# Linear attention with an MLP: q's features by a transpose of the first product instead of a second product, from unit 8 on

## The chip, the cores and the metric

The kernel runs on one core of a Trainium2 chip. The metric is the device time of one execution in microseconds (us). Before the change it is 369.69 us, the median of three runs (369.42 to 370.6).

## The reference

```
proj = q @ w_phi                      # 8 batches, 8 heads, 576 tokens, 64 -> 128 features; k the same
proj = proj - max |proj|              # a maximum of each token
q_p, k_p = [exp(proj), exp(-proj)]    # 256 features each
kv = k_p^T v;  z = sum of k_p over the tokens
x = (q_p kv) / (q_p z + 1e-6)         # heads side by side: 8 x 576 x 512
xn = (x - mean) / sqrt(var + 1e-6) * g_ln
out = x + relu(xn @ w_ch1) @ w_ch2    # 512 -> 2048 -> 512
```

Inputs and output are float32. The kernel multiplies in bfloat16 and sums in float32.

## The kernel before, in words

**Units and pairs.** The eight batches form four pairs. A pair has eight units, one for two heads of one batch, so there are 32 units, numbered 0 to 31, and units 8 to 31 belong to pairs 1 to 3. The 576 tokens of a head are four tiles of 128 and a tail of 64; the two heads of a unit make eight full tiles and one mixed tile. When the attention of a pair is far enough, its 1152 tokens (nine tiles of 128) go through the layer norm and the MLP in three groups of tiles: (4, 3, 2) in pairs 0 to 2, (3, 3, 3) in pair 3. The first group needs the pair's first four units, the others the second four.

**A unit of attention.** q and k are cast to bfloat16 and transposed, for the first eight units on TensorE and later by a DMA transpose of nine tiles on SP's queue (`a_trans_dma`, L755; its issue is L791, its result `qkT`). Then three kinds of products with `w_phi` follow:

- `main_products` (L880, the products at L885 and L891): tokens on the partitions, features along the row, for k and for q. `maxima` (L948, reduce at L953) takes the maximum of each token on DVE. For k, two exps on ACT (L967) make the features `EB`; for q only the maximum was needed.
- `tail_products` (L896, the products at L900), which the change speaks of as the second product: q again, with features on the partitions and tokens along the row. Two exps on ACT (L1033) make `EA`, the form in which the numerator needs q's features.
- `a_mixed` (L803): the mixed tile, in both forms, with exps of its own (L835, L839).

From unit 4 on (`tiled`) the products of the first two kinds use 64 of TensorE's 128 rows, since a head has 64 dimensions, and are issued in groups by `a_group` (L919) that take both A banks of PSUM at once. Two units share three groups: g1 has k and q of the even unit, g2 the even unit's second product and the odd unit's k, g3 the odd unit's q and its second product. An A bank is 1024 float32 wide. It comes free when its last reader is done: k's after the second exp, q's first product after the maximum, the second product after its second exp.

Then POOL scales v by exps of the maxima (`scale_main`, L974), `a_kv` (L1051, products at L1059 and L1065) sums k's features times v, and `a_num` (L1100, products at L1125, L1133 and L1139) makes numerator and denominator in two parts; part 0 takes an A bank from pair 1 on. DVE scales and adds (L1155, L1161) and inverts (L1167), and POOL writes the quotient into `x` (L1242, L1175; the first units write from DVE). `x` has three buffers, one for each pair in turn.

**The MLP.** `x` is centred (L1330 on DVE, L1335 on ACT, L1340 on POOL) and transposed, in pair 0 on TensorE and from pair 1 on by a DMA transpose on SP's queue (`x_trans_dma`, L1290, issue L1296; its result `xT`). `first` (L1383, products L1389) multiplies by the first matrix, and a ReLU on ACT (L1400) or DVE (L1398) empties the B bank. `second` (L1449, products L1458) multiplies by the second matrix, and ACT (L1471) with POOL (L1477), or DVE alone (L1466), adds `x` and leaves an output tile for SP to store (L1362, L1371). `x` is thus read until a pair's last output tile is made.

**The order of the work.** Each engine, and SP's DMA queue, works through a fixed list in order. `Order.run` (L229) makes these lists when the program is built: every step has a planned duration, what it reads and writes, the PSUM banks that it takes or gives back, and a rank, which is how late it may start, counted back from the MLP's due times, plus an offset from the table `OFF` (L38) by stage and kind of step. Whenever an engine of the plan is free, it takes the ready step with the lowest rank. The first rows of `OFF` are for units 0 to 7 one by one, the others for spans of four units. In the plan a DMA transpose of n tiles holds SP for at least 1.3 us. While the plan has nothing for PE in its first 75 us, it puts in products of zeros (L1665), the filler.

Of the kernel before, what the change touches and what calls it, by code (L numbers as in the profile page):

```python
# [17 lines left out]
def bcast(ap: bass.AP, dim: int, n: int) -> bass.AP:  # L18
# [15 lines left out]
TILED = 4  # L34
FOLD = 4
# [4 lines left out]
        "load": 291.2, "trans": 484.1, "trans.copy": -195.4, "mixed": 341.2, "mixed.max": 116.4,  # L40
        "mixed.exp": 189.4, "mixed.fold": -404.3, "k": -3.8, "k.max": 215.0, "k.em": -118.9,
        "k.exp": 583.1, "en": -216.0, "vv": -100.4, "q": 65.3, "q.max": -159.0, "q.em": 255.7,
        "tails": 174.6, "tails.exp": -410.3, "kv": 6.5, "kv.copy": 79.0, "num0": 131.7,
        "num1": -968.2, "num.dve": -227.8, "g1": 0.0, "g2": 0.0, "g3": 0.0, "put": 717.2,
# [3 lines left out]
        "load": 291.2, "trans": 511.8, "trans.copy": -106.8, "mixed": 340.9,  # L48
        "mixed.max": -109.0, "mixed.exp": 164.3, "mixed.fold": -181.6, "k": -0.3,
        "k.max": -400.0, "k.em": -20.9, "k.exp": 125.3, "en": -151.3, "vv": -156.9, "q": -49.0,  # L50
        "q.max": 314.4, "q.em": 304.2, "tails": 151.0, "tails.exp": -391.2, "kv": 141.9,
        "kv.copy": -46.4, "num0": 0.7, "num1": 201.4, "num.dve": -650.0, "g1": 0.0, "g2": 0.0,
        "g3": 0.0, "put": -13.8, "ln": 223.3, "w1": -144.2, "w2": -136.8, "ln.c": -23.8,
        "ln.t": -23.8,
    },
    {
        "load": 291.2, "trans": 438.4, "trans.copy": 145.2, "mixed": 324.3, "mixed.max": -85.1,
        "mixed.exp": 161.8, "mixed.fold": 14.6, "k": -20.8, "k.max": -401.0, "k.em": 78.2,
        "k.exp": -37.2, "en": -240.5, "vv": -112.4, "q": 149.6, "q.max": -212.7, "q.em": 595.0,
        "tails": -126.8, "tails.exp": -55.8, "kv": -164.2, "kv.copy": -20.3, "num0": -1.2,  # L60
        "num1": 340.4, "num.dve": -181.6, "g1": 0.0, "g2": 0.0, "g3": 0.0, "put": 44.6,
        "ln": -23.8, "w1": -144.2, "w2": 20.3, "ln.c": -23.8, "ln.t": -23.8,
    },
    {
        "load": 291.2, "trans": 101.5, "trans.copy": -4.0, "mixed": 268.3, "mixed.max": -90.8,
        "mixed.exp": 90.4, "mixed.fold": 174.0, "k": 8.8, "k.max": -396.2, "k.em": 243.2,
        "k.exp": -294.7, "en": -302.0, "vv": -102.0, "q": -15.0, "q.max": 52.5, "q.em": 236.8,
        "tails": 368.4, "tails.exp": -384.7, "kv": 383.3, "kv.copy": -55.5, "num0": 431.0,
        "num1": -539.1, "num.dve": -231.8, "g1": 0.0, "g2": 0.0, "g3": 0.0, "put": 225.4,
        "ln": -14.1, "w1": -144.2, "w2": -136.8, "ln.c": 107.3, "ln.t": 102.1,  # L70
    },
    {
        "load": 316.8, "trans": 376.2, "trans.copy": -87.1, "mixed": 51.8, "mixed.max": -100.8,
        "mixed.exp": 164.7, "mixed.fold": -36.7, "k": 556.5, "k.max": 202.3, "k.em": 295.2,
        "k.exp": -167.4, "en": -276.9, "vv": -79.3, "q": 110.5, "q.max": 328.5, "q.em": 303.8,
        "tails": 326.2, "tails.exp": -216.9, "kv": 149.0, "kv.copy": 26.7, "num0": 833.5,
        "num1": -731.1, "num.dve": -351.0, "g1": 137.0, "g2": 17.7, "g3": -5.0, "put": 614.2,
# [3 lines left out]
        "load": 6.3, "trans": -355.5, "trans.copy": -99.1, "mixed": 457.5, "mixed.max": 103.0,  # L81
        "mixed.exp": 265.5, "mixed.fold": 170.2, "k": -2.1, "k.max": -335.5, "k.em": -146.7,
        "k.exp": 597.3, "en": 0.0, "vv": -167.9, "q": 84.5, "q.max": 451.8, "q.em": 568.9,
        "tails": 184.4, "tails.exp": -231.7, "kv": -244.6, "kv.copy": -5.9, "num0": 974.5,
        "num1": -583.9, "num.dve": -219.9, "g1": -233.9, "g2": -41.7, "g3": 81.5, "put": -107.6,
        "ln": 61.6, "w1": -341.2, "w2": -67.5, "ln.c": 107.2, "ln.t": 107.2,
    },
    {
        "load": 544.7, "trans": 446.6, "trans.copy": 285.4, "mixed": 170.0, "mixed.max": -148.7,
        "mixed.exp": 58.0, "mixed.fold": -156.9, "k": -85.8, "k.max": 114.2, "k.em": 74.9,  # L90
        "k.exp": 606.5, "en": -36.5, "vv": -101.1, "q": -87.9, "q.max": 444.8, "q.em": 402.4,
        "tails": 124.7, "tails.exp": -331.1, "kv": 122.4, "kv.copy": 30.0, "num0": 311.2,
        "num1": 336.1, "num.dve": -226.1, "g1": -219.3, "g2": 21.1, "g3": -5.0, "put": 133.8,
# [3 lines left out]
        "load": 6.3, "trans": 477.2, "trans.copy": 113.9, "mixed": 187.6, "mixed.max": 54.3,  # L97
        "mixed.exp": 95.1, "mixed.fold": -78.3, "k": -1.2, "k.max": 94.8, "k.em": 77.7,
        "k.exp": -15.1, "en": -138.5, "vv": -247.2, "q": 144.6, "q.max": 497.6, "q.em": 422.9,
        "tails": 71.6, "tails.exp": -522.1, "kv": 195.5, "kv.copy": 46.4, "num0": -350.3,  # L100
        "num1": 476.8, "num.dve": -367.6, "g1": -233.9, "g2": -41.7, "g3": 9.4, "put": 654.8,
        "ln": 128.4, "w1": -341.2, "w2": -67.5, "ln.c": 9.3, "ln.t": -13.2,
    },
    {
        "load": 1027.4, "trans": 380.0, "trans.copy": 96.2, "mixed": 111.5, "mixed.max": 134.0,
        "mixed.exp": 110.2, "mixed.fold": 0.0, "k": -33.5, "k.max": -381.2, "k.em": 18.8,
        "k.exp": -168.2, "en": -391.8, "vv": 44.3, "q": -27.3, "q.max": 345.4, "q.em": 507.3,
        "tails": -210.6, "tails.exp": -450.0, "kv": 243.2, "kv.copy": 27.1, "num0": -273.7,
        "num1": -948.7, "num.dve": -230.0, "g1": -19.8, "g2": 109.3, "g3": -3.1, "put": -48.3,
        "ln": 89.4, "w1": -0.3, "w2": 28.2, "ln.c": 244.7, "ln.t": 81.2,  # L110
    },
    {
        "load": 208.4, "trans": 545.4, "trans.copy": 96.2, "mixed": 258.5, "mixed.max": -56.2,
        "mixed.exp": 324.3, "mixed.fold": 0.0, "k": -33.5, "k.max": 271.0, "k.em": 2.2,
        "k.exp": -25.0, "en": -24.6, "vv": 34.8, "q": -27.3, "q.max": 127.1, "q.em": 396.1,
        "tails": -210.6, "tails.exp": -364.6, "kv": 110.1, "kv.copy": 113.5, "num0": 862.2,
        "num1": -917.2, "num.dve": -255.0, "g1": -187.1, "g2": 88.1, "g3": 12.2, "put": 673.2,
        "ln": 152.9, "w1": -0.3, "w2": 28.2, "ln.c": -85.7, "ln.t": -194.5,
    },
    {  # L120
        "load": 349.4, "trans": 518.2, "trans.copy": 96.2, "mixed": 425.7, "mixed.max": 80.5,
        "mixed.exp": -148.7, "mixed.fold": 0.0, "k": -33.5, "k.max": -335.1, "k.em": 251.5,
        "k.exp": 606.2, "en": -344.7, "vv": -52.8, "q": -27.3, "q.max": 694.0, "q.em": 266.8,
        "tails": -210.6, "tails.exp": -189.3, "kv": 74.7, "kv.copy": 113.9, "num0": 862.5,
        "num1": -563.0, "num.dve": 88.2, "g1": -402.2, "g2": 9.2, "g3": -1.7, "put": 184.1,
        "ln": 261.4, "w1": 1888.2, "w2": 28.2, "ln.c": -170.7, "ln.t": 175.5,
    },
    {
        "load": 2.9, "trans": 573.2, "trans.copy": 96.2, "mixed": 346.8, "mixed.max": 104.5,
        "mixed.exp": 306.5, "mixed.fold": 0.0, "k": -33.5, "k.max": 269.3, "k.em": -29.5,  # L130
        "k.exp": -55.5, "en": -222.1, "vv": -186.3, "q": -27.3, "q.max": 915.3, "q.em": 361.1,
        "tails": -210.6, "tails.exp": -365.1, "kv": 139.5, "kv.copy": 109.0, "num0": 247.1,
        "num1": -828.1, "num.dve": -407.2, "g1": -439.6, "g2": -36.1, "g3": -36.0, "put": 676.4,
        "ln": 38.6, "w1": -0.3, "w2": 28.2, "ln.c": -59.9, "ln.t": -23.9,
    },
    {
        "load": 391.2, "trans": 283.5, "trans.copy": 96.2, "mixed": 259.4, "mixed.max": -96.2,
        "mixed.exp": 255.9, "mixed.fold": 0.0, "k": -33.5, "k.max": -330.9, "k.em": 159.3,
        "k.exp": 583.5, "en": -154.8, "vv": -175.0, "q": -27.3, "q.max": -199.2, "q.em": 271.6,
        "tails": -210.6, "tails.exp": -130.9, "kv": -301.6, "kv.copy": 10.8, "num0": 625.0,  # L140
        "num1": -826.7, "num.dve": -353.8, "g1": -249.2, "g2": -18.9, "g3": -127.1,
        "put": 122.0, "ln": 159.7, "w1": -441.2, "w2": 28.2, "ln.c": -39.7, "ln.t": 107.9,
    },
# [1562 lines left out]
```

## Time and profile before

| | |
|---|---|
| median of three runs | 369.69 us |
| the profiled execution | 369.84 us |
| its span, first to last instruction | 367.8 us |
| TensorE's granted clock, mean | 0.999 |
| first MLP product (L1389) | 47.1 us after the span's start |
| bytes read from HBM, written | 36.77 MB, 9.44 MB |

The profile is of one execution. PE stands for TensorE's products, PEld for its weight loads, DVE for VectorE, ACT for ScalarE, POOL for GpSimd, SP for SyncE, whose queue issues most DMAs. A row of the timeline has start, duration, engine, line, operation, what is written from what, its form and how many instructions were merged; in brackets stands the engine's idle time before it and what ended it. A product's duration holds its way through the array, so the next one starts before it ends: rates are read from start to start. A group's row has the union of its busy times, the mean duration in ns, and the idle time before its instructions. A row of a table of stretches has the stretch, its length, the busy time and the number of instructions of each engine, the granted clock, the DMA engines' mean share (packets of one engine can overlap, so it can pass 1) and GB/s.

### The profile page before, as it was taken

Reading aid. Unit: us, or ns where it says so; the run is one execution under the profiler, and the core shown is the slowest. Engines: PE = TensorE matmul, PEld = TensorE weight load, DVE = VectorE, ACT = ScalarE, POOL = GpSimd, SP = SyncE. Lnnn points to the kernel's source line nnn. Section 1 sums busy time; section 2 is a strip of 40 time slices with the busy share of each in tenths; the row PEclk is TensorE's granted clock in tenths of the full one; section 3 lists DMA queues with packets and bytes.
Section 4 is the critical chain, followed back from the end, with each engine's and each line's share of the span. In section 5 each row is a group of like instructions: output and inputs, shape, how many; then the busy total and the mean of one; then the engine's idle time right before and its main releaser. Section 6 shows DMA issues by size and latency. Waiting matters only on the chain.

```text
span 367.8 us, 9571 instructions
## 1 busy us (share of the span) xinstructions
PE 357.9 (97%) x3673; PEld 223.4 (61%) x3673; DVE 249.9 (68%) x572; ACT 266.5 (72%) x583; POOL 211.7 (58%) x368
## 2 busy tenths in 40 slices
PE   8889899999999999999999999999999999999996
PEld 8788765556576555555666645455666665555544
DVE  4677887798889969878989857987797754000001
ACT  3789978669899977794979686957787666444430
POOL 4449537787867397666778775747557263110111
PEclk9999999999999999999999999999999999999999
DMA  7999999979976678579667443671403003400012
GB/s 201 315 221 258 230 246 261 258 181 297 217 130 210 129 212 177 177 110 219 189 189 114 131 91 101 80 178 64 87 6 71 30 31 75 102 29 29 30 57 86
DMA packets 92141, 53.50 MB, mean 145 GB/s; under 512 B 58544, under 2 KB 87536, under 8 KB 92096
## 3 DMA queue, kind: packets, MB, share of 16 engines
q1 hardware_dynamic: 87056, 47.86, 53.6%
q0 software_dynamic: 4416, 4.49, 7.2%
q8 instruction: 28, 0.46, 0.5%
q10 hardware_dynamic: 624, 0.56, 0.5%
q14 instruction: 17, 0.14, 0.1%
HBM read 36.77 MB, written 9.44 MB: 126 GB/s over the span
## 4 chain that ended last, share of the span: by engine, by line
PE 84%; DVE 6%; ACT 5%; DMA 3%; issue 1%; DVEq 0%; ACTq 0%
PE b_bank L1389 31%; PE b_bank L1458 30%; PE n_bank L1665 4%; PE n_bank L1065 4%; PE a_bank L891 3%; DMA qkT<-b 3%; PE a_bank L1133 2%; PE a_bank L900 2%; DVE m L953 2%; PE n_bank L1059 1%; ACT ea L1033 1%; ACT hT_all L1033 1%; PE b_bank L1423 1%; ACT hT_all L967 1%; PE n_bank L1133 1%
## 5 line engine op out<-in xcount | busy, mean ns | idle before, releaser
L1389 PE MATMUL b_bank<-xT,w 128*128 128x384 bf16 (+2 forms) x768 | 148.2, 326 | 0.9 <-ACT hT_all L1400 0.9
L1458 PE MATMUL b_bank<-w,hT_all 128*128 128x512 bf16 x560 | 144.6, 379 | 0.0
L1389 PEld LDWEIGHTS <-w 128*128 128x128 bf16 x768 | 71.2, 98 | 53.5 <-issue 1.9
L1400 ACT ACTIVATE hT_all<-b_bank 128x384 bf16<-128x384 f32 (+2 forms) x123 | 60.3, 491 | 51.1 <-PE b_bank L1389 50.1
L953 DVE TENSOR_REDUCE m<-a_bank 128x8 f32<-128x1024 f32 x64 | 77.1, 1218 | 17.6 <-PE a_bank L891 11.8
L1458 PEld LDWEIGHTS <-hT_all 128*128 128x128 bf16 x560 | 50.3, 98 | 42.6 <-issue 1.3
L967 ACT ACTIVATE eb<-a_bank 128x1024 bf16<-128x1024 f32 x60 | 60.8, 1031 | 7.0 <-DVE m L953 3.5
L1033 ACT ACTIVATE ea<-a_bank 128x1024 bf16<-128x1024 f32 x60 | 60.0, 1036 | 3.2 <-PE a_bank L900 2.9
L977 POOL TENSOR_TENSOR vv<-v,em 128x512 bf16<-128x512 f32 x30 | 31.5, 1049 | 44.8 <-ACT em L958 34.2
L1477 POOL TENSOR_TENSOR o<-o,x 128x512 f32<-128x512 f32 x23 | 26.5, 1154 | 51.6 <-ACT o L1471 46.2
L1398 DVE TENSOR_SCALAR hT_all<-b_bank 128x384 bf16<-128x384 f32 (+2 forms) x69 | 38.5, 560 | 14.3 <-PE b_bank L1389 12.3
L1242 POOL TENSOR_TENSOR x<-numc,rden 128x384 bf16<-128x384 f32 (+1 forms) x56 | 34.2, 617 | 22.6 <-DVE rden L1167 20.3
L977 POOL TENSOR_TENSOR vv<-v,en 128x512 bf16<-128x512 f32 x30 | 31.4, 1045 | 0.2
L1466 DVE SCALAR_TENSOR_TENSOR o<-b_bank,rstd,x 128x512 f32<-128x512 f32 x12 | 8.9, 744 | 29.1 <-PE b_bank L1458 29.1
L1310 DVE BATCH_NORM_STATS2 st<-x 128x6 f32<-128x256 bf16 (+1 forms) x68 | 26.8, 426 | 2.6 <-POOL x L1242 2.3
L1471 ACT ACTIVATE o<-b_bank,rstd 128x512 f32<-128x512 f32 x23 | 15.9, 691 | 17.4 <-PE b_bank L1458 17.2
L1133 PEld LDWEIGHTS <-ea 128*128 128x128 bf16 x448 | 21.6, 97 | 6.8
L1065 PE MATMUL n_bank<-vv,eb 128*128 128x65 bf16 x480 | 25.2, 194 | 0.0
L1665 PE MATMUL n_bank<-wz 128*128 128x120 bf16 x307 | 23.9, 228 | 1.0 <-DVE KV L1073 1.0
L772 POOL TENSOR_TENSOR b<-qk,one 128x1024 bf16<-128x1024 f32 x13 | 24.6, 1892 | 0.5 <-DMA qkT<-b 0.3
L1065 PEld LDWEIGHTS <-eb 128*128 128x128 bf16 x480 | 20.9, 98 | 3.8
L1665 PEld LDWEIGHTS <-wz 128*128 128x128 bf16 x308 | 20.0, 105 | 2.3 <-issue 1.3
(131 smaller groups left out, 502.2 us busy)
## 6 DMA issues: line engine op xcount, KB each, us to landing
out_dram<-o SPq DMA_DIRECT2D x31, 256.0 KB, 2.5
qk<-in_k_dram SPq DMA_DIRECT2D x12, 512.0 KB, 5.8
qk<-in_q_dram SPq DMA_DIRECT2D x12, 512.0 KB, 6.8
v<-in_v_dram SPq DMA_DIRECT2D x12, 512.0 KB, 4.8
w<-in_moe_w_ch_dram POOLq DMA_DIRECT2D x8, 512.0 KB, 11.8
qk<-in_k_dram SPq DMA_DIRECT2D x8, 256.0 KB, 7.3
qk<-in_q_dram SPq DMA_DIRECT2D x7, 256.0 KB, 7.6
v<-in_v_dram SPq DMA_DIRECT2D x7, 256.0 KB, 7.0
```

Source lines behind the costliest of these rows:

```text
L953: nc.vector.reduce_max(out=m, in_=ps, axis=AX.X, apply_absolute_value=True)
L967: nc.scalar.activation(eb, ps, AF.Exp, scale=(1.0, -1.0)[t])
L977: nc.gpsimd.tensor_tensor(out=u["vv"][:, t, 0:MX, 0:D], in0=vb[:, hh, :].rearrange("p (c d) -> p c d", d=D), in1=bcast(e[:, 0:MX], 2, D), ...
L1033: nc.scalar.activation(u["EA"][:, t, 0:1024], u["pt"], AF.Exp, scale=(1.0, -1.0)[t])
L1065: nc.tensor.matmul(ps[:, t, c // 4, :], EB[:, t, c, :], vv[:, t, c, :], start=False, stop=(t == 0 and c == MX - 1), skip_group_check=True,)
L1133: nc.tensor.matmul(ps[t][:, i, :], ea(u, t, c), KV[:, t, c // 4, :], start=True, stop=True,)
L1242: nc.gpsimd.tensor_tensor(out=x_, in0=num, in1=rd, op=ALU.mult)
L1389: nc.tensor.matmul(st["ps"], w1_sb[:, kc, jj * P : (jj + 1) * P], xT_bufs[(pair * NR + r) % XB][:, kc : m * KC : KC, :], start=(kc == 0), ...
L1398: nc.vector.tensor_relu(h_sb, st["ps"])
L1400: nc.scalar.activation(h_sb, st["ps"], AF.Relu)
L1458: nc.tensor.matmul(ch[t], hT[r, jj][:, rt * P : (rt + 1) * P], w2_sb[:, jj, :], start=(jj == 0), stop=(jj == JC - 1),)
L1665: nc.tensor.matmul(banks[res][i][:, 0:WN] if res else warm, wz, wz[:, 0:WN], start=bool(res), stop=bool(res), skip_group_check=True,)
```

## The change

- **q's features** (units 8 to 31, `turned`). Two exps on ACT (`exps_q`) read q's first product and write tokens by features into a new buffer `QE` (two of them, one for each second unit). A DMA transpose of 16 tiles on SP's queue (`turn_features`) turns them into `EA`. The second product and its exps are gone for these units. q's maximum now comes behind the two exps and releases the A bank.
- **Groups.** Each of these units has one group, g1 with k and q, and its own call of `a_mixed`; g2 and g3 are left for units 4 to 7.
- **Layout of `EA`.** One row of 20 tiles, with the two signs' main tiles first, and the numerator's view `ea` finds its tile by unit.
- **k's first exp** in units 0 to 3 (`early`) is planned ahead of the maximum, which waits for it; both were free to start before.
- **`x` has two buffers** instead of three. The quotients of a pair wait in the plan for the last residual of the pair two before (`x left`).
- **The table `OFF`** has new numbers for most entries, units 0 to 7 too.

```diff
+TURNED = 8
...
-    xpool = ctx.enter_context(tc.tile_pool(name="xpool", bufs=3))
+    xpool = ctx.enter_context(tc.tile_pool(name="xpool", bufs=2))
...
-        eb = consts.tile([P, 2, (MX + 2) * P], BF16, name=f"ea{i}")
-        nc.vector.memset(eb[:, :, MX * P :], 0.0)
+        eb = consts.tile([P, 2 * (MX + 2) * P], BF16, name=f"ea{i}")
+        nc.vector.memset(eb[:, 2 * MX * P :], 0.0)
...
+    qe_bufs = [consts.tile([P, 2, MX, F], BF16, name=f"qe{i}") for i in range(2)]
...
+    def early(n):
+        return n < 4
+
+    def turned(n):
+        return n >= TURNED
...
+        def exps_q(t):
+            nc.scalar.activation(
+                qe_bufs[n % 2][:, t].rearrange("p (c h) f -> p h c f", h=2),
+                u["pm", 0].rearrange("p (h c) f -> p h c f", h=2), AF.Exp, scale=(1.0, -1.0)[t],
+            )
+
+        def turn_features():
+            def turn():
+                nc.sync.dma_start_transpose(
+                    out=u["EA"][:, 0 : 2 * MX * P].rearrange("p (c f) -> p c f", f=P),
+                    in_=qe_bufs[n % 2].rearrange("p t c f -> p (t c f)"),
+                )
+
+            dma("SP", rk("tails", n), 0, turn, r=[("QE", 0, n % 2), ("QE", 1, n % 2)],
+                w=[("EA", 0, n % 2), ("EA", 1, n % 2)], tiles=2 * MX)
...
+        if not i and turned(n):
+            for t in range(2):
+                add("ACT", 0.92, rk("tails.exp", n), lambda t=t: exps_q(t), r=[ps_key, ("QE", 0, n % 2)],
+                    w=[("QE", t, n % 2)])
+            turn_features()
+        read = [ps_key]
+        if i and early(n):
+            add("ACT", 0.92, rk("k.exp", n), lambda: exps(0), r=[ps_key], w=[("EB", 0, slot(n))])
+            read.append(("EB", 0, slot(n)))
+        elif not i and turned(n):
+            read += [("QE", t, n % 2) for t in range(2)]
-        add("DVE", 1.14, rk(nm + ".max", n), maxima, r=[ps_key], w=[("m", i, n % 4)],
+        add("DVE", 1.14, rk(nm + ".max", n), maxima, r=read, w=[("m", i, n % 4)],
             release=None if i else ("A", 1))
...
     def ea(u, t, c):
-        o = (c % 2) * 512 + (c // 2) * P if c < MX else c * P
-        return u["EA"][:, t, o : o + P]
+        if c >= MX:
+            o = 2 * (MX + t) * P + (c - MX) * P
+        elif turned(u["n"]):
+            o = (t * MX + c) * P
+        else:
+            o = t * MX * P + (c % 2) * 512 + (c // 2) * P
+        return u["EA"][:, o : o + P]
...
+        rd += [("x left", pair - 2)]
         add("POOL", 0.15 + 0.22 * ht, V_put, puts, r=rd,
...
-                add("POOL", op, RELU, residual, r=[], w=[ok])
+                add("POOL", op, RELU, residual, r=[], w=[ok, ("x left", pair)])
...
-            if not tiled(n) or n % 2 == 0:
+            if not tiled(n) or n % 2 == 0 or turned(n):
                 a_mixed(u)
             if not tiled(n):
                 a_main(u, 1)
-            elif n % 2 == 0:
+            elif n % 2 == 0 or turned(n):
                 a_group("g1", ("k", u), ("q", u))
...
-        elif n < NU and n % 2:
+        elif n < NU and n % 2 and not turned(n):
             a_group("g3", ("q", u), ("t", u))
...
-        if n < NU and tiled(n) and n % 2 == 0:
+        if n < NU and tiled(n) and n % 2 == 0 and not turned(n):
             a_mixed(units[n + 1])
             a_group("g2", ("t", u), ("k", units[n + 1]))
```

More of the change, by code (lines that the diff above doesn't have):

```diff
@@ L72 @@
-    {
[L73 to L77, printed above, removed]
+        "load": 291.2, "trans": 587.1, "trans.copy": 91.6, "mixed": 268.9, "mixed.max": -236.4,
@@ L136 @@
-    {
[L137 to L142, printed above, removed]
+        "load": 6.3, "trans": 520.9, "trans.copy": 155.2, "mixed": 310.4, "mixed.max": -83.0,
@@ L1014, in a_main @@
             return
[L1016 to L1017 removed]
+        if not early(n):
+            add("ACT", 0.92, rk("k.exp", n), lambda: exps(0), r=[ps_key, ("m", i, n % 4)],
+                w=[("EB", 0, slot(n))])
         add("ACT", 0.92, rk("k.exp", n), lambda: exps(1),
```

148 lines of the change are left out of this document (77 added, 71 removed).

## The prediction

> **What bounds the kernel now.** I read the page's busy times first, then a table of five stretches, then TensorE's timeline, because a busy PE need not be a PE that does useful work. The page, whole span:
>
> ```profile
> PE 357.9 (97%) x3673; PEld 223.4 (61%) x3673; DVE 249.9 (68%) x572; ACT 266.5 (72%) x583; POOL 211.7 (58%) x368
> ```
>
> The stretches (length, then busy time of each engine, granted clock, DMA share), and below them the filler products (L1665) alone in the first two:
>
> ```profile
> 0.00:47.00 47.00, 41.69 (x704) 37.68 (x705) 33.54 (x92) 37.23 (x71) 26.88 (x52) 1.00 1.07 245
> 47.00:100.00 53.00, 52.14 (x534) 30.59 (x532) 42.68 (x91) 41.46 (x93) 39.16 (x64) 1.00 1.05 240
> 100.00:200.00 100.00, 99.93 (x1038) 60.28 (x1037) 86.83 (x200) 83.95 (x190) 72.14 (x127) 1.00 0.71 172
> 200.00:300.00 100.00, 100.00 (x1037) 59.88 (x1034) 78.38 (x169) 75.31 (x175) 61.43 (x114) 1.00 0.37 83
> ...
> 0.00:47.00 47.00, 20.79 (x275) 17.71 (x276) 1.00 1.07 245
> 47.00:100.00 53.00, 3.38 (x37) 2.29 (x34) 1.00 1.05 240
> ```
>
> Up to 47 us PE half fills its time with filler and waits for data. From 47 us on it holds 37 fillers and 0.86 us of idle, and from 100 us on nothing but the program's products, at clock 1.00. So what is taken off PE after 74 us, where the first changed unit starts, shortens the run by as much, as long as MLP products are ready to move up. TensorE's timeline tells whether the products are also closely packed, and what one attention group costs:
>
> ```profile
> 110.26 0.62 PE L891 MATMUL a_bank<-wbk,qkT 64*128 64x128 bf16 x16
> 110.81 0.61 PE L1458 MATMUL b_bank<-w,hT_all 128*128 128x512 bf16 x2
> ...
> 120.03 0.81 PE L1458 MATMUL b_bank<-w,hT_all 128*128 128x512 bf16 x3
> 120.68 0.60 PE L1389 MATMUL b_bank<-xT,w 128*128 128x256 bf16 x4
> 121.11 0.81 PE L1458 MATMUL b_bank<-w,hT_all 128*128 128x512 bf16 x3
> 121.86 0.39 PE L900 MATMUL a_bank<-qkT,wbk 64*128 64x512 bf16 x2
> 122.08 0.39 PE L891 MATMUL a_bank<-wbk,qkT 64*128 64x128 bf16 x8
> 122.40 0.23 PE L1059 MATMUL n_bank<-vv,eb 128*128 128x130 bf16 x1
> ```
>
> From start to start three 128x512 products take 0.65 us (120.03 to 120.68), 0.217 us each: the queue is full. A group of q's second product and one first product (L900 x2, L891 x8) takes 122.40 - 121.86 = 0.54 us. The three products ahead of it take 0.75 us instead of 0.65, so entering the 64-row form costs 0.10 us more: 0.64 us a group. The group of k and q (L891 x16) takes 110.81 - 110.26 = 0.55, with the entry 0.65 us.
>
> **PE, the term that counts.** In units 8 to 31 two units now share three groups: k and q of the first; the first's second product with the second's k; q and the second product of the second. That is 12 x 3 = 36 groups. Afterwards each unit has one group of k and q: 24. Gone are 24 groups with a second product, 24 x 0.64 = 15.4 us; new are 12 of k and q, 12 x 0.65 = 7.8 us. PE saves 7.6 us. The busy column would have said more:
>
> ```profile
> L900 PE MATMUL a_bank<-qkT,wbk 64*128 64x512 bf16 x56 | 10.8, 381 | 0.0
> ```
>
> It gives 10.8 us for 28 units, 9.3 us for 24; I take the 7.6 us of the start times. The Trainium skill (Perfetto Trace Analysis, Identifying the Most-Contended Engine) says that matmul busy time is a poor measure because matmuls are pipelined: by that rule, too, 9.3 us is not to be had, and the sum would be 362.2 rather than 360.5 us.
>
> **ACT, DVE and the A banks.** Two exps of the second product (L1033) go, two of the first product (L967's form, output reordered in the same way) come; q's maximum (L953) stays but runs behind its exps.
>
> ```profile
> L953 DVE TENSOR_REDUCE m<-a_bank 128x8 f32<-128x1024 f32 x64 | 77.1, 1218 | 17.6 <-PE a_bank L891 11.8 <-ACT hT_all L967 2.6 <-PE a_bank L885 1.8
> L967 ACT ACTIVATE eb<-a_bank 128x1024 bf16<-128x1024 f32 x60 | 60.8, 1031 | 7.0 <-DVE m L953 3.5 <-DVE rden L1167 2.6 <-PE a_bank L885 0.7
> L1033 ACT ACTIVATE ea<-a_bank 128x1024 bf16<-128x1024 f32 x60 | 60.0, 1036 | 3.2 <-PE a_bank L900 2.9
> ```
>
> ACT: 4 x 1.03 us a unit before and after, so nothing. DVE: 2 x 1.22 us, nothing. The new wait of q's maximum queues ReLUs and numerators behind it on DVE, and whoever wants the A bank behind those. But k's maximum (1.22) runs beside q's exps (2.06) and q's maximum beside k's exps, so a group holds its banks some 4.1 us, two units 8.2 us. Now it is 3.3 (k and q), 4.1 (second product and k) and 2.1 (q and second product), 9.5 us. The banks get easier, and I count no cost. The new indexing of EA and the memset cost nothing: same instructions, same sizes.
>
> **k's first exp ahead of the maximum, units 0 to 3.** The order is there already, here for unit 3 (ACT, DVE, ACT):
>
> ```profile
> 22.79 1.02 ACT L967 ACTIVATE hT_all<-a_bank 128x1024 bf16<-128x1024 f32 x1
> ...
> 23.84 2.36 DVE L953 TENSOR_REDUCE m<-a_bank 128x8 f32<-128x1024 f32 x2 [0.79 <-ACT hT_all L967]
> ...
> 25.10 1.02 ACT L967 ACTIVATE hT_all<-a_bank 128x1024 bf16<-128x1024 f32 x1 [0.95 <-DVE m L953]
> ```
>
> The maximum waits for the first exp, the second exp for the maximum. Where a unit has it the other way round, at most one maximum, 1.2 us, moves either way. The new offsets reorder units 0 to 7 as well. No row shows by how much the first MLP product shifts; I take 0, with 2 us to either side (about that 1.2 us twice).
>
> **The transposes.** Each changed unit adds one of 16 tiles on SP's queue. The nearest rows are the transposes of x (8 to 16 tiles) and of q and k (9 tiles):
>
> ```profile
> L1296 SPq DMA_TRANSPOSE xT<-xc x9: 1232/1466/3068, 124.6 to 313.0; - x9
> DMA to landing us min/median/max: 3.1/3.7/5.5
> ...
> L791 SPq DMA_TRANSPOSE qkT<-b x24: 1242/1338/4563, 63.5 to 257.2; - x24
> L813 PE MATMUL n_bank<-wbk,qkT x24: 272/273/283, 74.3 to 290.9; 128*128 128x256 bf16 x24
> DMA to landing us min/median/max: 3.2/3.6/9.7
> ```
>
> So q's features land 3.1 to 9.7 us after the issue; I take 5.5, the slowest transpose of x, since the 16-tile ones are x's largest. A unit takes (290.9 - 74.3) / 23 = 9.4 us and QE and EA are double, so the landing is later but not slower than the units. It costs nothing while the MLP has work of an earlier group. On SP's queue it is some 1.5 us, 24 times, 35 us in all, with output stores, loads, x's row moves and the next q and k transposes queued behind. Loads go out four units ahead, so 1.5 us is covered there.
>
> ```profile
> 306.90:311.50 4.60, 4.60 (x28) 2.55 (x27) 2.39 (x8) 2.66 (x6) 1.07 (x1) 1.00 0.46 86
> ...
> 80.00:300.00 220.00, 219.07 (x2271) 132.07 (x2271) 181.83 (x402) 177.20 (x403) 149.50 (x268) 1.00 0.58 137
> ```
>
> In the first stretch only a 12-tile transpose of x runs: 0.46 x 4.60 = 2.1 us of the DMA engines, 2.8 us for 16 tiles, 68 us for 24. Over 80 to 300 us the share goes from 0.58 to about 0.89. The stretch before 100 us already ran at 1.05, so this has room on the mean, none up to 100 us.
>
> **x in two buffers.** Pair 2 may write x only when pair 0's last output is made, pair 3 when pair 1's is. Last output of pairs 0 and 1 (DVE), first write for pairs 2 and 3 (POOL):
>
> ```profile
> 138.43 0.74 DVE L1466 SCALAR_TENSOR_TENSOR o<-b_bank,rstd,x 128x512 f32<-128x512 f32 x1
> 231.48 0.74 DVE L1466 SCALAR_TENSOR_TENSOR o<-b_bank,rstd,x 128x512 f32<-128x512 f32 x1
> ...
> 169.82 1.18 POOL L1242 TENSOR_TENSOR x<-numc,rden 128x384 bf16<-128x384 f32 x2
> 244.61 0.40 POOL L1242 TENSOR_TENSOR x<-numc,rden 128x128 bf16<-128x128 f32 x1 [2.03 <-DVE rden L1167]
> ```
>
> Slack 30.7 and 12.4 us: no cost. Were it gone, POOL's queue would stand at the write with v's scaling behind it, and attention with it.
>
> **The sum.** The profiled execution took 369.84 us, 2.0 more than its span and 0.15 above the median of 369.69. 369.84 - 7.6 = **362.2 us**. Next late is again PE.
>
> **Rivals.** Within 0.3% (1.1 us) of before counts as no change, about what a measurement here can tell.
>
> *Attention does not speed up with PE (0.16).* MLP groups start soon after their x lands. The tightest late one, x's transpose and its first product:
>
> ```profile
> 306.97 1.31 SPq L1296 DMA_TRANSPOSE xT<-xc  x1
> 314.60 1.46 PE L1389 MATMUL b_bank<-xT,w 128*128 128x384 bf16 x8
> ```
>
> Landed by the median at 306.97 + 3.7 = 310.7. With 7.6 us saved PE wants it at 307.0; if ACT, DVE and the longer way of q hold attention to its old pace, PE waits 3.7 us: 365.9 us. Against it: ACT and DVE are at 75% and 78% between 200 and 300 us.
>
> *The new order also closes holes (0.08).* After 47 us there are 0.86 us idle and 37 fillers at some 0.05 us from start to start, 2.8 us: 359.4 us.
>
> *Attention keeps its pace and the first 100 us get worse (0.05).* 365.9 plus 2.7 us or more of a later first MLP group, 368.6 to 370.8 us: no change.
>
> *ACT stands behind transposes, and the run gets slower (0.08).* One such case is there, up to 100 us:
>
> ```profile
> 84.62 3.62 SPq L791 DMA_TRANSPOSE qkT<-b  x1
> 94.31 1.04 ACT L770 CAST b<-qk 128x1024 bf16<-128x1024 f32 x1 [1.42 <-DMA qkT<-b]
> 95.79 2.11 PE L1389 MATMUL b_bank<-xT,w 128*128 128x384 bf16 x12 [0.86 <-ACT hT_all L1400]
> ```
>
> A cast waits for a buffer that a slow transpose still reads, the ReLU behind it on ACT is late, and PE loses 0.86 us. The new exps wait in the same way for QE, and the numerators for EA. It decides from (7.6 + 1.1) / 0.86, 10 of the 24 units on; half of them give 362.2 + 12 x 0.86 = 372.5 us. Against it: QE has two buffers, 18.8 us of time for a landing of 9.7 at most.
>
> *The transposes become the bound (0.01).* If tiles passed one by one at the worst rate here, 9.7 / 9 = 1.08 us, 16 would take 17.2 us and a unit with its q and k 27 us against 9.4: 24 x 27 = 648 us for them alone. The median, 3.6 us for 9 tiles, speaks against it. The Trainium skill (VectorE: DVE Perf Modes, The three transpose paths) gives 1309 ns for a 128x128 transpose by DMA against 390 ns on TensorE and prefers TensorE where PSUM will do; 16 in a row would be an estimated 21 us. The landing row contradicts that rate for many tiles in one transpose.
>
> **How the numbers follow.** The forecast has 0.62 at 362.2, about 360.2 to 364.2. The range 359.4 to 367.0 takes in the closed holes and the old pace with 1.1 us of loss at the start, and leaves 0.14 out. Faster: 0.62 + 0.16 + 0.08 = 0.86; same 0.05; slower 0.08 + 0.01 = 0.09.
>
> **What would show it.** L900 down to 16 products, 24 groups of L891 x16 at 0.55 us after 74 us; no filler and no PE idle after 100 us; the new transposes landing in 4 to 6 us; the last MLP group starting some 7 us earlier. PE idle at the first products of a group, ended by x's transpose, would show the first rival; ACT idle ended by a DMA of EA or QE the slow one. A first MLP product well off 47 us would prove the start wrong.

## The result, and the profile after

The changed kernel takes 374.39 us (median of six runs, 371.43 to 376.54), and the kernel before, run between them on the same chip, 369.97 us (six runs, 369.42 to 370.63). The ratio is 1.0117, with a 95% interval of 1.0073 to 1.0162: slower by 4.4 us, where 7.6 us less had been forecast. The profiled execution of the changed kernel is the longest of its six, 376.54 us, with a span of 374.4 us against 367.8 before.

The page's busy times and DMA slices, then the table of stretches (length, busy time of each engine, granted clock, DMA share, GB/s), all of after:

```profile
PE 353.6 (94%) x3670; PEld 227.1 (61%) x3712; DVE 254.2 (68%) x571; ACT 265.5 (71%) x587; POOL 208.9 (56%) x363
...
DMA  7999999799999999999899999889456515200012
```

```profile
47.00:100.00 53.00, 49.43 (x557) 30.30 (x559) 47.72 (x97) 42.49 (x96) 36.09 (x65) 1.00 1.05 223
100.00:200.00 100.00, 93.35 (x930) 56.86 (x940) 78.47 (x172) 79.56 (x180) 66.41 (x111) 1.00 1.01 222
200.00:300.00 100.00, 96.92 (x1016) 60.65 (x1029) 82.30 (x181) 77.12 (x186) 64.27 (x119) 1.00 0.84 166
...
200.00:250.00 50.00, 47.34 (x493) 28.45 (x498) 40.01 (x91) 36.99 (x90) 36.32 (x62) 1.00 1.02 202
```

PE is busy for 4.3 us less than before, as intended, in a span 6.6 us longer. From 47 to 300 us it now stands idle for 3.57 + 6.65 + 3.08 = 13.3 us, where it stood 0.9 us before. The DMA share between 100 and 200 us has gone from 0.71 to 1.01, and between 200 and 300 us from 0.37 to 0.84: the mean that the prediction named for 80 to 300 us (0.89) came out at 0.94, and the share stays near or above 1 until 250 us.

**A ledger of the two spans**, from the first MLP product on. One row of stretches for before, one for after, and for each the filler products behind the first MLP product:

```profile
47.10:300.00 252.90, 251.97 (x2599) 150.65 (x2597) 207.79 (x457) 200.71 (x455) 172.72 (x303) 1.00 0.65 151
...
47.10:100.00 52.90, 3.28 (x35) 2.19 (x32) 1.00 1.05 240
```

```profile
48.00:300.00 252.00, 238.83 (x2482) 147.10 (x2512) 207.62 (x446) 198.18 (x456) 166.60 (x293) 1.00 0.95 200
...
48.00:100.00 52.00, 4.32 (x45) 3.00 (x45) 1.00 1.05 223
```

The first MLP product starts at 48.0 us, 0.9 later. From there to the span's end it is 326.4 us against 320.7: 5.7 us longer. Up to 300 us the idle time of PE has grown by 13.2 - 0.9 = 12.3 us (behind 300 us it is 3.7 us before and 4.0 after) and filler by 1.0 us, so the program's own products must have become about 12.3 + 1.0 - 5.7 = 7.6 us shorter, which is the prediction's term. (A part of the idle time may not be real: the page has 42 products fewer than weight loads, and a product without a record shows as a hole. The one-tile kernel below, whose stretch has no such gap between products and weight loads, is the cleaner measure of this term.)

**What PE waits for.** The waits of after, those on a DMA (engine, tile and line that waited; total us, times, longest):

```profile
POOL b L773 <- DMA qkT<-b: 13.2, 6, 3.4
...
ACT b L771 <- DMA qkT<-b: 10.3, 7, 2.8
...
PEld L1173 <- DMA ea<-qe: 6.8, 4, 2.4
...
DVE b L764 <- DMA qkT<-b: 3.5, 3, 1.6
...
PE a_bank L1173 <- DMA ea<-qe: 3.0, 2, 1.9
...
PE n_bank L1173 <- DMA ea<-qe: 2.6, 2, 2.0
...
PE b_bank L1430 <- DMA xT<-xc: 1.3, 1, 1.3
```

(L773, L771 and L764 of after are the casts of q and k on POOL, ACT and DVE; L1173 the numerator's products; L984 the new transpose, L792 the one of q and k, L1337 that of x.) PE waits four times for the new transpose, 5.6 us, and once for x's, 1.3 us; the weight loads' 6.8 us are the same four waits. All waits of PE of 0.2 us and more between 47 and 300 us add up to 11.3 us; 6.9 of them are for these transposes, 0.6 for a ReLU on ACT. The casts of q and k at the three lines wait 27.0 us for a buffer that the transpose of an earlier unit has not yet read; before, POOL and ACT waited 1.5 and 1.4 us in this way. Late casts make late products, so a part of PE's remaining idle time, which the view puts down to DVE, ACT and POOL, may start there too.

The new transposes as the tile view of `ea` has them, and one of the four waits in the timelines of ACT (the second exp of q's features of that unit), SP and PE:

```profile
L984 SPq DMA_TRANSPOSE ea<-qe x24: 1363/2997/6958, 74.7 to 295.9; - x24
...
DMA to landing us min/median/max: 4.2/5.2/10.0
```

```profile
109.17 1.04 ACT L977 ACTIVATE qe<-a_bank 128x1024 bf16<-128x1024 f32 x1
```

```profile
112.85 0.50 SPq L569 DMA_DIRECT2D qk<-in_q_dram  x1
113.44 1.27 SPq L569 DMA_DIRECT2D vx<-in_v_dram  x2
114.76 0.60 SPq L569 DMA_DIRECT2D v<-in_v_dram  x1
115.47 6.96 SPq L984 DMA_TRANSPOSE ea<-qe  x1
122.47 2.80 SPq L792 DMA_TRANSPOSE qkT<-b  x2
125.37 0.62 SPq L1130 DMA_DIRECT2D x<-xs  x1
```

```profile
121.94 0.60 PE L1430 MATMUL b_bank<-xT,w 128*128 128x256 bf16 x4
124.42 0.54 PE L1173 MATMUL a_bank<-KV,ea 128*128 128x65 bf16 x12 [1.88 <-DMA ea<-qe]
124.80 0.60 PE L1499 MATMUL b_bank<-w,hT_all 128*128 128x512 bf16 x2
```

The features are complete at 110.21 us, but nine loads stand ahead of their transpose in SP's list and go out until 115.36 us. The transpose then holds SP's queue for 6.96 us, and its data are there at 124.4, 8.9 us after its issue and 14.2 us after the features were complete. PE comes to the numerator some 1.9 us too early and waits. The next thing in PE's list is an MLP product that needs none of this and starts, without a wait, right behind the numerator; the last ReLU ahead of it on ACT ended at 123.45 us, so what it reads was there while PE still waited. SP's rows abut: the next issue begins 0.05 us after the transpose has let go. Over all 24 units, the time from the end of the second exp (L977) to the issue of the transpose (L984) is 3.9 us by the median and up to 9.0, and to the landing 9.4 us by the median and up to 16.5. So the view's 5.2 us, which starts at the issue, is little more than half of how late the features come.

### The profile page after: what moved, and what is told of

The parts are those of the page before. It is cut to its first block, busy times and chain, and to the rows that moved or that the text cites. A ratio compares the mean times of both kernels' runs of the same rounds, so it can differ in the third digit from the quotient of the medians.

```text
span 374.4 us, 9633 instructions
## 1 busy us (share of the span) xinstructions
PE 353.6 (94%) x3670; PEld 227.1 (61%) x3712; DVE 254.2 (68%) x571; ACT 265.5 (71%) x587; POOL 208.9 (56%) x363
## 4 chain that ended last, share of the span: by engine, by line
PE 52%; DMA 26%; DVE 8%; issue 4%; POOL 4%; ACT 3%; SPq 2%; DVEq 0%; POOLq 0%; ACTq 0%
PE b_bank L1430 22%; PE b_bank L1499 19%; DMA qk<-in_q_dram 9%; DMA ea<-qe 7%; DMA qkT<-b 6%; DMA qk<-in_k_dram 2%; PE n_bank L1105 2%; PE a_bank L898 2%; SPq L569 2%; DVE m L960 2%; PE a_bank L1173 2%; DMA xT<-xc 2%; DVE b L769 2%; POOL vv L1000 1%; POOL b L773 1%
## 5 line engine op out<-in xcount | busy, mean ns | idle before, releaser
L1499 PE MATMUL b_bank<-w,hT_all 128*128 128x512 bf16 x522 | 138.0, 379 | 1.9 <-issue 0.3
L1441 ACT ACTIVATE hT_all<-b_bank 128x384 bf16<-128x384 f32 (+2 forms) x129 | 63.2, 496 | 48.1 <-PE b_bank L1430 47.7
L1518 POOL TENSOR_TENSOR o<-o,x 128x512 f32<-128x512 f32 x21 | 24.4, 1160 | 54.7 <-ACT o L1512 53.7
L977 ACT ACTIVATE qe<-a_bank 128x1024 bf16<-128x1024 f32 x48 | 48.6, 1031 | 6.0 <-PE a_bank L898 5.3
L1439 DVE TENSOR_SCALAR hT_all<-b_bank 128x512 bf16<-128x512 f32 (+2 forms) x63 | 34.4, 552 | 8.2 <-PE b_bank L1430 4.5
L1507 DVE SCALAR_TENSOR_TENSOR o<-b_bank,rstd,x 128x512 f32<-128x512 f32 x14 | 10.5, 747 | 35.3 <-PE b_bank L1499 32.3
L1173 PEld LDWEIGHTS <-ea 128*128 128x128 bf16 x448 | 22.0, 97 | 17.7 <-DMA ea<-qe 6.8
L773 POOL TENSOR_TENSOR b<-qk,one 128x1024 bf16<-128x1024 f32 x12 | 22.7, 1892 | 14.9 <-DMA qkT<-b 13.2
L1706 PE MATMUL n_bank<-wz 128*128 128x120 bf16 x365 | 27.6, 226 | 0.1
L1706 PEld LDWEIGHTS <-wz 128*128 128x128 bf16 x395 | 24.7, 103 | 1.5 <-issue 0.3
L1512 ACT ACTIVATE o<-b_bank,rstd 128x512 f32<-128x512 f32 x21 | 14.4, 687 | 11.5 <-PE b_bank L1499 10.8
```

The lines of the kernel that those rows point to most:

```text
L977: nc.scalar.activation(qe_bufs[n % 2][:, t].rearrange("p (c h) f -> p h c f", h=2), u["pm", 0].rearrange("p (h c) f -> p h c f", h=2), AF. ...
L1173: nc.tensor.matmul(ps[t][:, i, :], ea(u, t, c), KV[:, t, c // 4, :], start=True, stop=True,)
L1439: nc.vector.tensor_relu(h_sb, st["ps"])
L1441: nc.scalar.activation(h_sb, st["ps"], AF.Relu)
L1499: nc.tensor.matmul(ch[t], hT[r, jj][:, rt * P : (rt + 1) * P], w2_sb[:, jj, :], start=(jj == 0), stop=(jj == JC - 1),)
L1706: nc.tensor.matmul(banks[res][i][:, 0:WN] if res else warm, wz, wz[:, 0:WN], start=bool(res), stop=bool(res), skip_group_check=True,)
```

## The experiments

The letters in the expectations: theory A is that the 24 new transposes of 16 tiles do the harm, since they run into the loads and each other on DMA engines and SP's queue that were nearly full, and what they deliver or hold up comes late for a PE list made for earlier arrival. Rival B is that the new order, made with the new offsets, is the fault. Rival C is that `x` in two buffers is. Each kernel was timed beside the kernel before on the same chip.

### One tile in place of sixteen, in the same order

```diff
-                    out=u["EA"][:, 0 : 2 * MX * P].rearrange("p (c f) -> p c f", f=P),
-                    in_=qe_bufs[n % 2].rearrange("p t c f -> p (t c f)"),
+                    out=u["EA"][:, 0:P].rearrange("p (c f) -> p c f", f=P),
+                    in_=qe_bufs[n % 2][:, 0, 0, :],
```

> The changed kernel with every engine's order kept, but each new transpose turns one tile of the 16 (15 of 16 tiles of q's main features keep stale values, so the numbers that come out are not the reference's). Theory A, the transposes' DMA time: the transposes fill the DMA engines up to 250 us, features and casts come later than planned, and PE stands in its fixed order. Then most of the 13 us of PE idle after 47 us goes, the DMA share between 100 and 200 us falls from 1.01 to some 0.75, and the time is 361 to 365 us. Theory B, the order: the new lists of the engines and the 24 extra places on SP's queue are worse in themselves. Then the time stays at 371 to 375 us.

Measured: 363.69 us (363.32 to 365.19), 0.9833 of before (0.9810 to 0.9857), 6.4 us less. The lists, the offsets, the exps, the groups and the two buffers are those of after. The row of stretches from the first MLP product on, and the tile view of `ea`:

```profile
45.80:300.00 254.20, 252.45 (x2617) 154.87 (x2616) 215.64 (x470) 205.16 (x470) 172.19 (x303) 1.00 0.70 156
```

```profile
L984 SPq DMA_TRANSPOSE ea<-qe x24: 1109/1152/3806, 72.0 to 281.6; - x24
...
DMA to landing us min/median/max: 2.2/3.3/8.0
```

PE idles for 1.75 us in place of 13.2, and no wait in it ends with a transpose of q's features or of x. From the first MLP product to the end it is 361.2 - 45.8 = 315.4 us, 5.3 less than before, with 0.8 us more idle time and the same 1.0 us more of filler as after: the products have become 7.1 us shorter. So the order and the smaller PE work are worth what was forecast, within half a microsecond. From the first MLP product to the end after takes 326.4 us and this kernel 315.4: moving the other 15 tiles costs 11.0 us there, and 10.7 by the medians. The first MLP product itself is 2.2 us earlier than in after. That can't come from the new transposes, the first of which goes out at 72 to 75 us; up to there the two kernels are the same program.

### Eight tiles in place of sixteen, in the same order

```diff
+                    out=u["EA"][:, 0 : MX * P].rearrange("p (c f) -> p c f", f=P),
+                    in_=qe_bufs[n % 2][:, 0].rearrange("p c f -> p (c f)"),
```

> The changed kernel with the order kept, each new transpose turning 8 of its 16 tiles (the exps of minus q keep stale values, so the numbers are not the reference's). Theory A, the harm comes where SP's queue and the DMA engines are full, so it is not in proportion to the tiles: the queue is busy some 85 per cent between 100 and 200 us instead of 97, PE idle after 47 us is 2 to 6 us, and the time is 364 to 367 us, nearer to one tile (363.7) than to sixteen (374.4). Each tile costs alike: 369 us.

Measured: 364.55 us (363.59 to 365.28), 0.9838 (0.9807 to 0.9869). Half of the tiles cost 0.9 us over one tile, the other half 9.8. The stretch, and the tile view of `ea`:

```profile
100.00:200.00 100.00, 99.21 (x1002) 61.48 (x1015) 83.38 (x187) 86.57 (x196) 71.89 (x123) 1.00 0.98 210
```

```profile
L984 SPq DMA_TRANSPOSE ea<-qe x24: 1234/1386/3605, 72.4 to 282.6; - x24
```

The harm is not in proportion to the tiles, as if it started when something is full. At a DMA share of 0.98 from 100 to 200 us there is hardly any yet. SP's queue, its issues in the trace added up, is busy for 84% of 100 to 200 us here, for 76% with one tile, 94% in after and 48% before.

### Whole transposes, lighter loads, in the same order

```diff
-            ap=[[4 * D, P], [S * D, 2 * nu], [1, 4 * D]],
+            ap=[[4 * D, P], [S * D, 2 * nu], [1, D if n >= 8 else 4 * D]],
```

> The changed kernel with the order kept and all 24 transposes whole; each of the main loads of q, k and v for units 8 to 31 fetches a quarter of its bytes, in as many DMAs (the rest of the buffers keeps values of earlier units, so the numbers are not the reference's). Theory A in the form that loads and transposes together are too much for the DMA engines: without the loads' share the transposes are issued and land in time, SP's queue is busy some 75 per cent between 100 and 200 us, PE idle after 47 us is under 4 us, and the time is 362 to 366 us. Theory A in the form that 24 transposes of 16 tiles are too much for SP's queue whatever else moves: 370 to 375 us.

Measured: 363.77 us (363.68 to 365.29), 0.9830 (0.9807 to 0.9853). The stretch and the tile view:

```profile
100.00:200.00 100.00, 99.95 (x1021) 61.57 (x1021) 83.55 (x187) 86.33 (x196) 71.91 (x123) 1.00 0.87 165
```

```profile
L984 SPq DMA_TRANSPOSE ea<-qe x24: 1328/2238/3175, 72.0 to 283.9; - x24
...
DMA to landing us min/median/max: 4.3/4.5/6.2
```

All 16 tiles are moved, and yet nothing is lost against one tile. The longest hold falls from 6.96 to 3.18 us and the longest landing from 10.0 to 6.2; from the end of the second exp to the landing it is now 4.8 us by the median in place of 9.4, with hardly any wait ahead of the issue (0.03 us by the median in place of 3.9). This kernel and the first leave one half of the pair in place each, and both are fast: the transposes alone do no harm, the loads alone do none, the two together cost some 10 us. No cast waits for the transposes of q and k in any of these three kernels.

### Transposes that nobody waits for, in the old order

This kernel, and those of the two headings that follow, have before's offsets and its order for units that are not turned. Here no unit is turned, and a further transpose of 16 tiles, from a constant into a buffer that nobody reads, goes out behind each DMA transpose of q and k.

```diff
+TURNED = 32
...
+            nc.sync.dma_start_transpose(
+                out=qe_bufs[n % 2].rearrange("p t c f -> p (t c) f"),
+                in_=w2_sb[:, 0:4, :].rearrange("p j f -> p (j f)"),
+            )
```

> The kernel before with x in two buffers and the new layout, its order on PE, DVE, ACT and POOL kept, and on SP one more transpose of 16 tiles behind each of the 24 of q and k, from the second weight matrix to a buffer that nobody reads. Theory A: DMA time alone does harm: the share between 100 and 200 us goes from 0.71 to about 1.0, the transposes of q and k and of x land later, casts wait for them, and the run takes 373 to 380 us, slower than before by 1 to 3 per cent. Theory A2, only the numerators' new wait for a transpose does harm: 369 to 371 us. Theory B: also 369 to 371 us.

Measured: 391.50 us (390.00 to 392.43), 1.0573 (1.0547 to 1.0598). The stretch and a shorter one in it, then a row of ACT's timeline and one of PE's:

```profile
100.00:200.00 100.00, 89.88 (x878) 51.92 (x878) 75.68 (x174) 73.93 (x167) 62.24 (x107) 0.95 1.02 220
...
102.50:112.00 9.50, 5.53 (x31) 2.69 (x31) 3.03 (x9) 5.70 (x11) 3.75 (x6) 0.50 1.00 198
```

```profile
104.98 1.04 ACT L772 CAST b<-qk 128x1024 bf16<-128x1024 f32 x1 [7.99 <-DMA qkT<-b]
```

```profile
106.47 0.80 PE L1435 MATMUL b_bank<-xT,w 128*128 128x384 bf16 x2 [7.43 <-ACT hT_all L1446]
```

This is the chain of the prediction's slow rival in one place: a cast on ACT waits 7.99 us for a transpose to read its buffer, the ReLU (L1446) behind it in ACT's list is late by as much, and PE stands for 7.43 us with no free B bank. It loses 21.4 us against before though it has no wait of its own on the added transposes. The transposes' load suffices to slow the kernel. The loss is larger than theory A's 373 to 380 us; a part of it may be TensorE's clock, which is 0.50 around this hole; how much that adds was not separated.

### `x` in two buffers alone

```diff
+TURNED = 32
...
     def early(n):
-        return n < 4
+        return False
```

with the offsets of before.

> The change without its turned units, without the new order of k's first exp and with the old offsets: what is left is x in two buffers, the wait for the last residual and the new layout of the features. All engines' orders are those of before. Theory A and theory B: 369 to 371 us, no change, since writes of x come 12 to 30 us after the last read of their buffer. Theory C, the two buffers are what costs: 372 to 376 us.

Measured: 370.52 us (369.45 to 371.54, twelve runs), 1.0005 (0.9988 to 1.0022). The layout of `EA`, the two buffers of `x` and their wait cost nothing. Rival C falls.

### Fewer units turned, with before's offsets

```diff
-TURNED = 8
+TURNED = 24     # and 20, and 16
```

> Only units 24 to 31 are turned; offsets and the order of k's first exp as before, x in two buffers. Eight units save four groups, 4 x 0.64 = 2.6 us of PE. In the kernel before the DMA share is 0.37 between 200 and 300 us, where these units run. Theory A, transposes are harmless where DMA engines and SP's queue have room: 366.5 to 368.5 us, no PE idle after 200 us. Theory B, a new order without fitted offsets costs by itself: 369 to 373 us.

> Units 20 to 31 are turned, otherwise as the kernel that turns from unit 24 on. Six groups less, 3.9 us of PE. Theory A: most of the loads are through when unit 20 runs (after 190 us), so 365.5 to 368 us; if the last loads still collide, 368 to 370. Theory B: 369 to 373 us.

> Units 16 to 31 are turned, offsets as before. Eight groups less, 5.1 us of PE: 364.9 us if the transposes find room. Theory A: units 16 to 19 run from 160 to 200 us, where loads still go at 0.7 of the DMA engines, and 8 of the 16 tiles did no harm there, so 365 to 368 us; if they collide, 368 to 372 us. Theory B has nothing to add.

| units turned | median us (range) | ratio | 95% | DMA share 150–200, 200–250 |
|---|---|---|---|---|
| 24 to 31 | 368.18 (367.09–371.20) | 0.9947 | 0.9914–0.9979 | 0.68, 0.69 |
| 20 to 31 | 365.96 (365.42–368.87) | 0.9889 | 0.9852–0.9925 | 0.71, 0.84 |
| 16 to 31 | 368.94 (368.13–370.24) | 0.9959 | 0.9942–0.9977 | 1.00, 0.84 |

Twelve units, where the loads thin out, gain 4.1 us, about 0.3 us a unit as in the forecast (7.6 / 24). Four more, in the stretch from 150 us, which they fill to a share of 1.00, gain less, not more. The tile view of `ea` for units 20 to 31:

```profile
L985 SPq DMA_TRANSPOSE ea<-qe x12: 1317/2052/5102, 189.5 to 292.8; - x12
...
DMA to landing us min/median/max: 4.3/4.6/7.9
```

With units 20 to 31 the kernel beats both kernels, at 365.96 us. For units 16 to 31 the picture is not clean: PE's longest waits behind 100 us are for DVE and ACT, 1.3 and 0.8 us, none for a transpose, and each number of units has an order of its own. That the full stretch is why it gains less is argued, not shown.

### The offsets and the order

Three kernels change the order and keep the whole transposes. The first is after with before's table `OFF`; the second is after, with its own table and `early`, for units 20 to 31 only; the third tells the plan that the new transposes land 4 us later, so that the lists are remade.

```diff
 # first: OFF of before, all else as after
...
 # second
-TURNED = 8
+TURNED = 20
...
 # third
-            packets, ns, lag = tiles * 8 + BARRIER / 0.018, 0.018, LAND_T + sched.slack[2]
+            packets, ns, lag = tiles * 8 + BARRIER / 0.018, 0.018, LAND_T + sched.slack[2] + more
...
+                w=[("EA", 0, n % 2), ("EA", 1, n % 2)], tiles=2 * MX, more=4.0)
```

> The changed kernel with the table of offsets of before, and so with other lists on all engines. Theory A: transposes and loads are the same in number, so it is slower than before too, 373 to 385 us. Theory B, the new offsets are the fault: 362 to 368 us.

> Units 20 to 31 are turned, with the new offsets and the new order of k's first exp. With the old offsets the same kernel took 365.96 us. Theory A: the number of transposes beside loads decides, the offsets little: 365 to 368 us, first MLP product near 48 us. If the new offsets are worse for the units that still have a second product: 368 to 375 us.

> The changed kernel, in whose plan a turn of q's features lands 4 us later than it assumed; nothing else is edited, but every list is made anew. Theory A: the numerators come later in PE's list, the 5.6 us that PE waits for q's features go, other waits stay in part: 366 to 372 us. Theory B says nothing on the direction: 370 to 378 us, as any new order without fitted offsets.

Measured: 379.93 us (375.16 to 380.53), 1.0212 (1.0156 to 1.0267); 381.51 us (380.26 to 382.68), 1.0299 (1.0275 to 1.0323); 380.82 us (377.69 to 383.06), 1.0273 (1.0228 to 1.0317). The first says that the new offsets are not what makes after slow: without them it is no faster. The clean test of rival B is the one-tile kernel, which has after's order and is fast; there it falls. The other two kernels missed what theory A expected, and came out above the other range given for them too. In the second the same twelve units that gain 4.1 us with before's offsets lose 11.1 us. A row of its PE timeline shows the largest hole, ended by a mixed tile's exp on ACT, in a stretch where no unit is turned yet; the rows of ACT below it show why that exp was late, and the last row the granted clock around it:

```profile
96.25 0.29 PE L1099 MATMUL n_bank<-vv,eb 128*128 128x130 bf16 x1 [5.08 <-ACT ea L840]
...
94.37 1.04 ACT L771 CAST b<-qk 128x1024 bf16<-128x1024 f32 x1 [3.63 <-DMA qkT<-b]
95.91 0.29 ACT L840 ACTIVATE ea<-n_bank 128x128 bf16<-128x128 f32 x1
...
91.00:104.00 13.00, 7.06 (x56) 4.79 (x55) 7.06 (x18) 8.17 (x22) 7.23 (x14) 0.50 0.66 158
```

The exp stands behind a cast that waited 3.63 us for a transpose of q and k: the chain of the idle-transpose kernel again, here with no new transpose near it. So theory A alone, the number of new transposes beside loads, doesn't give the time of a kernel: for these twelve units after's table (and `early`) makes it 15 us longer than before's table does, and from 91 to 104 us its granted clock is 0.50. In the third kernel no wait for `ea` is left on PE, which is what the later landing was to do, but PE now waits 3.7 us for transposes of x, and whether planning for the true landing helps is not settled by it.

### The second sign by a reciprocal

exp(-x) is 1 / exp(x), so one exp, a transpose of 8 tiles and a reciprocal on DVE could make `EA`; the plan gave the reciprocal 1.1 us.

```diff
+                nc.vector.reciprocal(out=u["EA"][:, MX * P : 2 * MX * P], in_=u["EA"][:, 0 : MX * P])
```

> All 24 units turned, but only the features exp(q): one exp on ACT and 8 tiles turned instead of two and 16; the features exp(-q) are their reciprocal, one DVE instruction of 128 x 1024 on the turned tiles, planned at 1.1 us (no row shows one of this size). The lists are made anew with the new offsets. Theory A: the DMA side is that of the kernel that turns 8 tiles (364.6 us), ACT gets 25 us less and DVE 26 us more, some 93 per cent busy between 100 and 200 us: 364 to 370 us, no PE wait for turned features. If the reciprocal takes over 2 us, DVE becomes the bound: over 375 us.

Measured: 494.88 us (491.30 to 495.32), 1.3341 (1.3298 to 1.3384). The group of the reciprocals:

```profile
L991 DVE RECIPROCAL ea<-ea 128x1024 bf16<-128x1024 bf16 x24 | 156.9, 6536 | 0.2 <-DMA ea<-qe 0.2
```

At 6.5 us each they add 157 us to DVE and make it the bound.

## Why the prediction was wrong

- **PE's term, 7.6 us: right.** The ledger gives 7.6 us for after, an upper value since records are missing there, and 7.1 for the one-tile kernel, which runs 6.4 us faster than before.
- **ACT, DVE, the A banks and `x` in two buffers at nothing: right.** With the transposes made light, or the loads, the same order has no such loss; two buffers alone give 1.0005.
- **The landing, 5.5 us taken from a span of 3.1 to 9.7: right, but it is not the whole delay.** From the issue it is 5.2 by the median, 10.0 at most. Ahead of the issue the transpose stands behind loads and stores in SP's list, which the sum left out: the prediction has these queued behind the transposes, not the transposes behind them. From complete features to landed ones it is 9.4 us by the median.
- **"It costs nothing while the MLP has work of an earlier group": the step that failed.** The MLP had such work, and at 124.80 us it starts right behind the wait. PE works through a list that was fixed when the program was built, so a late `EA` stops the MLP products that stand behind the numerator: 5.6 us of PE in four waits, and with x's transpose 6.9 of the 11.3 us of waits that the view names. All that comes of the other 15 tiles is 10.7 us, where the sum had nothing. The work that could cover a wait must stand ahead of the waiting instruction on its engine; the prediction asked only whether it exists.
- **"On SP's queue it is some 1.5 us, 24 times, 35 us": mis-sized.** It took the median of the short holds, which were seen with a queue half busy. The holds are 3.0 us by the median and up to 6.96; the 24 add up to 81 us (33 with one tile, 43 with eight, 56 with light loads). The longest stand behind runs of large loads, or of loads and output stores, and with lighter loads the longest is 3.18 us.
- **"This has room on the mean, none up to 100 us": the right number, read wrongly.** 0.58 plus 68 us of transposes in 220 gave 0.89, and 0.94 came out for the same stretch. But up to 250 us the share is 1.05, 1.01 and 1.02 stretch by stretch, with nothing to spare. The prediction's own table of before had 0.71 for 100 to 200 us, to which the same sum, at 2.8 us each 9.4 us, adds 0.30: 1.01. That this is just the measured share is partly luck, since one tile in each transpose already gives 0.83 there with the new order and eight give 0.98; the sum was a warning, not a measure.
- **The slow rival (0.08) named the mechanism.** ACT stands behind transposes, a ReLU comes late, PE stops: the idle-transpose kernel shows it at 104.98 and 106.47 us. It also named the numerators' wait for `EA`, which is the larger part in after (5.6 us, against 0.6 for a ReLU), but priced everything by one case of a cast at before's DMA load. Against it stood 18.8 us of time for a landing of 9.7 at most; with the time ahead of the issue the longest is 16.5.

Open are two things. The runs don't tell apart whether the DMA engines or SP's queue is full first: with eight tiles the share is 0.98 and SP at 84% and there is next to no harm, and in after both are higher. The idle-transpose kernel speaks for the DMA engines, with SP's queue also at 84% from 100 to 200 us, a share of 1.02 and the largest loss of these, but it has another order. And the first MLP product starts at 45.8, 46.4 and 48.0 us in the profiled executions of the one-tile, eight-tile and changed kernels, which are the same up to there (at 47.2 in the light-load kernel, whose lighter loads begin at 32.9); what moves it was not looked into.

## What to carry to other kernels

Before work is moved to DMA, add its DMA time to the share of each stretch, not to the mean of the run, and where a stretch comes to 1, look at what will wait there, the old transfers too. A share of 1 is not harm in itself: before ran at 1.07 and 1.05 up to 100 us, and from 47 us on PE idled for 0.9 us only. And count a transfer's delay from when its data are ready, not from its issue. In a kernel with fixed lists, work that is ready elsewhere covers a late arrival only where it stands ahead of the waiting instruction in that engine's list. Such a change can still pay in the part of the run whose loads are done: here units 20 to 31 alone gave 0.9889 where units 8 to 31 gave 1.0117.

## What the runs showed of the hardware

- A DMA transpose held the queue that issued it for longer with larger loads ahead of it: 16 tiles held SP's queue from 1.36 us to 6.96 us with whole loads, and at most 3.18 us with loads of a quarter.
- A transpose of 16 tiles landed in 4.2 us at best. The Trainium skill (VectorE: DVE Perf Modes, The three transpose paths) gives 1309 ns for one tile of 128x128 by DMA; in one transpose of many tiles this is no rate, since 16 times as much would be an estimated 21 us.
- DVE's reciprocal takes 6536 ns for 128x1024 in bfloat16, 6.4 ns for each element of a row; DVE's maximum over a block of that size takes 1.22 us in before.
- Around long holes in PE's work the granted clock was 0.50 for some ten microseconds: in the idle-transpose kernel from 102.1 to 112.3 us, around a hole of 7.43 us, and in the kernel that turns units 20 to 31 with after's table from 90.6 to 104.3 us, around one of 5.08 us. In after, two holes of 1.9 us left it at 1.00. In the kernel whose plan had the later landing, with holes of up to 2.3 us, it was 0.91 over a stretch, and the numerator's products took up to 247 ns each there, 193 by the median. What sets the clock was not tested.

```profile
100.00:200.00 100.00, 90.65 (x839) 53.55 (x834) 69.73 (x145) 74.08 (x169) 62.51 (x101) 0.91 1.02 217
```
